# Retention and soft-MoE on one core: k by tokens made on the chip for ten steps, two weight pairs in ring tiles

## The chip, the cores and the metric

One NeuronCore of a Trainium2 chip runs the whole program. The metric is device time in microseconds (us), shorter is better. The engines are TensorE (PE, matmuls and transposes), VectorE (DVE), ScalarE (ACT), GpSimd (POOL) and SyncE (SP), which issues all DMAs here. Matmul results land in eight PSUM banks, everything else lives in SBUF.

## What is computed

```
# attention: q, k, v of 4 batches x 8 heads x 768 tokens x 64
state = gamma[h] * state + outer(k[t], v[t])      # per batch and head, 64 x 64
y[t]  = scale * q[t] @ state
x = y as (3072 tokens, 512)
# soft mixture of experts: 8 experts, 4 slots each
logits = x @ phi                                  # 3072 x 32
d = softmax over tokens;  slot_input = d.T @ x    # 32 x 512
h = relu(slot_input[e] @ w1[e]); slot_out[e] = h @ w2[e]    # 512 -> 1024 -> 512
c = softmax over slots;   out = c @ slot_out      # 3072 x 512
```

All data is fp32. The inputs are 25 MB of q, k, v (k twice: transposed and by tokens) and 33.6 MB of weights; the output is 6.3 MB.

## The kernel before, in words

The recurrence is done in chunks of 128 tokens. A step (NSTEP is 24) is one chunk of one batch with all 8 heads; step i belongs to batch i % 4. The main loop runs over P, 12 pairs of steps 2P and 2P+1. A group g is four steps, so two P.

**Inputs of a step.** load_in(i) (L169) takes one of six input tiles (NIN, 8 KB per partition) and loads four blocks of 512 columns: kT (k with head dimension on partitions), qT, v by tokens, and kn, k by tokens. The last four steps need no kn, as no state follows them; the first two load theirs late (L420). The scores are kT against qT, the state update is kn against v.

**Order on PE in one P** (P from 1 on). carry_mm (L215): the old states times q, from P = 2 on. attend_mm (L232): masked scores times v, into banks Y0 and Y1. state_mm (L259): kn times v into bank S, until P = 9. natural_mm (L276): eight transposes of the step outputs to token order, into A2 and A3. In even P turn_mm (L329), in odd P dispatch_u (L349, into A0) and logits_mm (L292, into sm). Then score_mm (L200) of the next two steps: 2P+2 into A0 and A1, 2P+3 into A2 and A3. P = 0 has its own order (L458 to L470): score_mm(2), attend, state_mm(0), score_mm(3), natural_mm(0) into A0 and A1. Before the loop stand score_mm(0), attend of step 0 and score_mm(1), with a few warm matmuls.

**Other engines.** VectorE masks the scores (L212), copies half of the step outputs (L257) and adds the state (L274); for P = 0 and 1, where the state begins, it copies it (L272). ScalarE copies the other half (L256), the transposed outputs (natural_copy, L288) and does the exponentials. GpSimd multiplies q (L191) and v (L195) by decay factors in place, as soon as a step's inputs are there.

**Order of the work.** manual_schedule (L93) keeps each engine's instructions in the order in which the program names them. A tile of a pool is given again once its last reader is done, and the instruction that writes it next waits for that. SP is one such ordered queue: a DMA that waits for its tile holds those behind it.

**Weights.** The list of weight tiles (L146) is 16 tiles of w1 and 16 of w2, 1 MB each, in the order of their use. PACE[P] of them are asked for at the head of each P, before that P's two inputs. The pool big holds 13; from P = 10 on weights go into input tiles that the last steps leave (weight_pool, L445), and after the loop into big again, each as a hidden-layer matmul frees it. The PACE of before asks for 19 tiles in the loop. The ring (NRING, nine tiles of 4 KB per partition) holds masked scores, step outputs and other short-lived data.

**After the loop.** hidden(g, k) (L558) does the first expert layer in eight pieces and frees two weight tiles with each; load_weights(2) stands behind each. Then the second layer (L654 to L663) in three blocks of output columns, and finish (L620), in which the 3072 x 512 output is made and stored by twelve DMAs of 512 KB (L646).

Of the kernel before, what the change touches and what calls it, by code (L numbers as in the profile page):

```python
# [43 lines left out]
NRING = 9  # L44
PACE = (1, 1, 1, 1, 1, 2, 1, 1, 2, 2, 2, 4)

# [34 lines left out]
def retention_soft_moe_kernel(  # L81
# [44 lines left out]
    cnat = small("cnat", [128, NSTEP, NSLOT])  # L126
    sst = [small(f"sst{b}", [128, NPAIR, D]) for b in range(B)]

# [21 lines left out]
    def load_weights(n):  # L150
        for _ in range(n):
            if not weights:
                return
            which, e, k = weights.pop(0)
            t = large(weight_pool[0])
            if which == "w1":
                nc.sync.dma_start(t, w1[e // 2, k])
                w1t[e, k], w1t[e + 1, k] = t[:, 0:FF], t[:, FF:2 * FF]
            else:
                nc.sync.dma_start(t, w2[w2n[0]])  # L160
                w2n[0] += 1
                w = BLOCKS[k][1]
                for j in range(256 // w):
                    w2t[e + j, k] = t[:, j * NFC * w:(j + 1) * NFC * w]

    st = {}
    pr = {}

    def load_in(i):  # L169
        t = large(inp)  # L170
        st[i] = dict(kT=t[:, 0:512].rearrange("p (g t) -> p g t", t=C),
                     qT=t[:, 512:1024].rearrange("p (g t) -> p g t", t=C),
                     v=t[:, 1024:1536].rearrange("p (h e) -> p h e", e=D),
                     kn=t[:, 1536:2048].rearrange("p (h d) -> p h d", d=D))
        if i < 2:
            if i == 0:
                nc.sync.dma_start(t[:, 0:1024], in_[i, :, 0:1024])
                nc.sync.dma_start(kt[:, 0:K_FIRST], consts[:, 0:K_FIRST])
                nc.sync.dma_start(t[:, 1024:1536], in_[i, :, 1024:1536])
            else:  # L180
                nc.sync.dma_start(t[:, 0:1536], in_[i, :, 0:1536])
            st[i]["late"] = (t[:, 1536:2048], in_[i, :, 1536:2048])
        elif i >= NSTEP - B:
            nc.sync.dma_start(t[:, 0:1536], in_[i, :, 0:1536])
        else:
            nc.sync.dma_start(t, in_[i])

    def decay_q(i):
# [79 lines left out]
    def state_add(P):  # L268
        for k in range(2):
            d = sst[(2 * P + k) % B]  # L270
            if P < B // 2:
                nc.vector.tensor_copy(d, pr[P]["S"][:, k])  # L272
            else:
# [123 lines left out]
    def split_c(q):  # L397
# [4 lines left out]
        nc.vector.tensor_tensor(c4r[:, :, :, 1, :], cq, c4s[q][:, :, :, 0, :], ALU.subtract)  # L402
        c4T[q] = slot()

# [14 lines left out]
    load_in(2)  # L419
    for i in range(2):  # L420
        nc.sync.dma_start(*st[i]["late"])
    load_in(3)
# [12 lines left out]
    score_mm(1)  # L435
    score_mask(1)
    for P in range(NPP):
        last = P == NPP - 1
# [19 lines left out]
        if P == 0:  # L458
# [7 lines left out]
            score_mask(3)  # L466
            natural_mm(0, names=("A0", "A1"))
            natural_copy(0)
            decay_table(qtab, K_QT)
            continue  # L470
        carry_mm(P)
        if last:
            dispatch_u(g - 1, ["A0"])
            logits_mm(g, (0, 1))
        attend_mm(P)
        if last:
            break
        attend_copy(P)
        if P < NPP - B // 2:
            state_mm(P)  # L480
            state_add(P)
        natural_mm(P)
        natural_copy(P)
# [236 lines left out]
```

## Time and profile before

| | us |
|---|---|
| median of 3 runs | 166.05 |
| all runs | 166.58, 166.05, 164.49 |
| the profiled execution | 164.77 |
| its span (first to last instruction) | 163.0 |
| PE busy | 146.4 (90%) |
| weight loads on PE (PEld) | 108.4 (67%) |
| DVE, ACT, POOL busy | 88.2, 39.1, 57.5 |
| DMA | 64.63 MB, mean 396 GB/s |

The span is what the rows of the profile divide; the profiled execution's own time is 1.77 us longer. Busy time of PE is that of modelled, pipelined instructions: the duration of one matmul overlaps the next, so the distance between starts is what a matmul costs in a row of them.

### The profile page before, as it was taken

What the parts mean: (1) busy time and instruction counts of PE and PEld (TensorE: products, weight loads), DVE (VectorE), ACT (ScalarE), POOL (GpSimd) and SP (SyncE); (2) the same over time, 40 slices, a digit from 0 to 9 for tenths busy, and PEclk for the clock granted to TensorE, in tenths of its full rate; (3) what the DMA queues carried; (4) which work ended last, traced back from release to release, by engine and by line L of the source; (5) the groups of instructions that cost most, each with busy time, mean ns of one, the idle gap of its engine ahead of it and who ended that gap; (6) DMA issues with size and microseconds to landing.
All of it is one profiled execution on the core that took longest, in us unless ns stands there. A gap on an engine that the chain in (4) does not pass through costs nothing.

```text
span 163.0 us, 5416 instructions
## 1 busy us (share of the span) xinstructions
PE 146.4 (90%) x2378; PEld 108.4 (67%) x2378; DVE 88.2 (54%) x198; ACT 39.1 (24%) x91; POOL 57.5 (35%) x62
## 2 busy tenths in 40 slices
PE   8976999999999899999999899999999999998400
PEld 2556989997999599869997787743244666565200
DVE  0437547574758675967576748677420305662500
ACT  3000222324332133122412332422114001432300
POOL 0231476858496666383885460000000000000000
PEclk9999999999999999999999999999999999999965
DMA  4899999999999999999999999998999999999993
GB/s 138 322 422 408 420 418 422 414 424 416 416 418 416 414 420 416 420 418 416 413 412 419 417 416 420 416 390 292 402 422 428 430 414 416 418 396 415 418 420 124
DMA packets 10679, 64.63 MB, mean 396 GB/s; under 512 B 1184, under 2 KB 1568, under 8 KB 4256
## 3 DMA queue, kind: packets, MB, share of 16 engines
q1 hardware_dynamic: 10656, 64.29, 96.5%
q8 instruction: 18, 0.29, 0.7%
q14 instruction: 5, 0.04, 0.1%
HBM read 58.00 MB, written 6.29 MB: 394 GB/s over the span
## 4 chain that ended last, share of the span: by engine, by line
PE 62%; DMA 22%; SPq 3%; DVE 2%; POOL 2%; issue 2%; ACT 1%; DVEq 0%; ACTq 0%; POOLq 0%
DMA b<-in_x_dram 16%; PE A L205 10%; PE Y L237 9%; PE A L660 7%; PE A L281 6%; DMA out_dram<-b 6%; PE Y L563 4%; PE Y L228 4%; PE S L265 4%; PE sm L298 3%; PE A L563 2%; PE S L563 2%; PE A L355 2%; PE A L410 2%; DVE r L212 2%
## 5 line engine op out<-in xcount | busy, mean ns | idle before, releaser
L212 DVE TENSOR_TENSOR r<-A,kt 128x512 f32<-128x512 f32 x48 | 30.0, 684 | 22.3 <-PE A L205 22.3
L191 POOL TENSOR_TENSOR b<-b,qtab 128x512 f32<-128x512 f32 x20 | 25.7, 1283 | 26.4 <-DMA b<-in_x_dram 19.5
L195 POOL TENSOR_TENSOR b<-b,kt 128x512 f32<-128x512 f32 x24 | 24.6, 1044 | 12.6 <-DMA b<-in_x_dram 12.6
L205 PE MATMUL A<-b 64*128 64x128 f32 x384 | 25.7, 282 | 3.6 <-DMA b<-in_x_dram 2.4
L205 PEld LDWEIGHTS A<-b 64*128 64x128 f32 x384 | 23.1, 191 | 6.8 <-issue 4.1
L237 PE MATMUL Y<-r,b 128*64 128x128 f32 x368 | 23.0, 276 | 0.0
L237 PEld LDWEIGHTS Y<-r,b 128*64 128x64 f32 x368 | 19.8, 137 | 2.5 <-issue 2.0
L288 ACT COPY r<-A 128x512 f32<-128x512 f32 x23 | 12.4, 589 | 29.3 <-PE A L281 29.3
L660 PE MATMUL A<-b,r 128*32 128x128 f32 (+1 forms) x384 | 16.3, 311 | 0.3 <-DMA b<-in_w_dram 0.3
L660 PEld LDWEIGHTS A<-b,r 128*32 128x32 f32 x384 | 10.7, 109 | 6.5 <-issue 2.9
L281 PE MATMUL A<-kt,r 128*128 128x128 f32 x96 | 13.3, 280 | 0.8 <-ACT r L256 0.8
L281 PEld LDWEIGHTS A<-kt,r 128*128 128x128 f32 x96 | 10.2, 140 | 2.2 <-ACT r L256 1.2
L265 PE MATMUL S<-b 128*64 128x64 f32 x320 | 11.0, 222 | 0.0
L265 PEld LDWEIGHTS S<-b 128*64 128x64 f32 x320 | 10.7, 138 | 0.0
L228 PE MATMUL Y<-b,sst 64*64 64x128 f32 x304 | 10.6, 276 | 0.0
L257 DVE COPY r<-Y 128x512 f32<-128x512 f32 x9 | 6.2, 690 | 5.9 <-PE Y L237 5.9
L228 PEld LDWEIGHTS Y<-b,sst 64*64 64x64 f32 x304 | 8.2, 132 | 1.2
L387 POOL TENSOR_TENSOR cnat<-cnat,cz 128x128 f32<-128x128 f32 x6 | 2.4, 401 | 17.2 <-DVE cz L386 10.4
L298 PEld LDWEIGHTS sm<-r,phis 128*32 128x32 f32 x192 | 6.2, 110 | 3.3 <-issue 3.3
L563 PE MATMUL Y<-b,siT 128*32 128x512 f32 x64 | 8.2, 597 | 0.0
L298 PE MATMUL sm<-r,phis 128*32 128x128 f32 x192 | 7.4, 273 | 0.0
L379 ACT ACTIVATE cnat<-cnat 128x128 f32<-128x128 f32 x6 | 1.9, 310 | 23.0 <-DVE cnat L378 23.0
(133 smaller groups left out, 158.4 us busy)
## 6 DMA issues: line engine op xcount, KB each, us to landing
b<-in_w_dram SPq DMA_DIRECT2D x32, 1024.0 KB, 16.9
b<-in_x_dram SPq DMA_DIRECT2D x18, 1024.0 KB, 13.6
out_dram<-b SPq DMA_DIRECT2D x12, 512.0 KB, 9.7
b<-in_x_dram SPq DMA_DIRECT2D x5, 768.0 KB, 13.8
b<-in_x_dram SPq DMA_DIRECT2D x3, 256.0 KB, 8.9
b<-in_x_dram SPq DMA_DIRECT2D x1, 512.0 KB, 4.3
kt<-in_consts_dram SPq DMA_DIRECT2D x1, 136.0 KB, 4.2
kt<-in_consts_dram SPq DMA_DIRECT2D x1, 116.0 KB, 6.7
```

The lines of the kernel that those rows point to most:

```text
L191: nc.gpsimd.tensor_tensor(q, q, qtab, ALU.mult)
L195: nc.gpsimd.tensor_tensor(v, v, vsc[:, i // B, :].unsqueeze(2).broadcast_to([128, H, D]), ALU.mult)
L205: nc.tensor.matmul(s["sc"][r][:, g, :], s["kT"][half(r), g, :], s["qT"][half(r), g, :], start=True, stop=True, skip_group_check=True)
L212: nc.vector.tensor_tensor(s["A"][:, r], s["sc"][r], mask.unsqueeze(1).broadcast_to([128, NPAIR, C]), ALU.mult)
L228: nc.tensor.matmul(p["y"][k][b][half(half_of(r, g)), gl, :], sst[(2 * P + k) % B][half(r), g, :], s["qT"][half(r), g, :], start=(gl == 0 a ...
L237: nc.tensor.matmul(pr[P]["y"][k][g // 2][half(half_of(r, g)), g % 2, :], s["v"][:, 2 * g + r, :], s["A"][:, r, g, :], start=(P < B // 2 an ...
L265: nc.tensor.matmul(S_[half(r), k, g, :], s["kn"][:, 2 * g + r, :], s["v"][:, 2 * g + r, :], start=True, stop=True, skip_group_check=True)
L281: nc.tensor.transpose(X[k][:, g * 128:(g + 1) * 128], pr[P]["yT"][:, k, g, :], ident)
L288: (nc.scalar.copy if engines[k] == "scalar" else nc.vector.tensor_copy)(xn, pr[P]["X"][k])
L298: nc.tensor.matmul(q["ltp"][32 * j:32 * j + 32, :], phis[:, p, :], st[GRP * g + j]["yT"][:, p, :], start=(p == 0), stop=(p == NPAIR - 1), ...
L563: nc.tensor.matmul(hp[g][hf][32 * j:32 * j + 32, :], siT[:, k, :], w1t[4 * g + j, k][:, hf * 512:(hf + 1) * 512], start=(k == 0), stop=(k ...
L660: nc.tensor.matmul(op[32 * j:32 * j + 32, :w], hT[fc // 4][:, fc % 4, 4 * g + j, :], t[:, fc * w:(fc + 1) * w], start=(g == 0 and fc == 0) ...
```

## The change

For the ten steps in TURNED, kn is no longer loaded; four PE transposes turn kT into a PSUM bank and one ScalarE copy writes kn (turn_k). Steps 0 and 1 are turned before the loop, 2 and 3 in P = 0 around natural_copy(0), and 4, 6, 8, 10, 12 and 14 in P = 1 to 6, between the state update and natural_mm. PACE is another sequence: 13 tiles until P = 8, none in P = 9, two each in P = 10 and 11. In P = 11 two more weight tiles are loaded as four halves into ring tiles (load_halves), and two into input tiles. The four states become slices of one tile, which c4T[0] takes over later. The first states (P = 0 and 1) are copied by ScalarE instead of VectorE.

```
--- before.py
+++ after.py
@@ -42,7 +42,8 @@
 NBIG = 13
 NIN = 6
 NRING = 9
-PACE = (1, 1, 1, 1, 1, 2, 1, 1, 2, 2, 2, 4)
+PACE = (1, 1, 2, 1, 2, 1, 2, 1, 2, 0, 2, 2)
+TURNED = (0, 1, 2, 3, 4, 6, 8, 10, 12, 14)
 
 K_MASK, K_VSC, K_YT, K_FIRST = 0, 128, 176, 272
 K_ID, K_QT, K_GC, K_J, K_ALL = 272, 400, 496, 500, 504
@@ -124,7 +125,8 @@
     wsel = small("wsel", [128, NSLOT])
     siT = small("siT", [128, NK, NSLOT])
     cnat = small("cnat", [128, NSTEP, NSLOT])
-    sst = [small(f"sst{b}", [128, NPAIR, D]) for b in range(B)]
+    sall = small("sst", [128, B * NPAIR * D])
+    sst = [sall[:, b * NPAIR * D:(b + 1) * NPAIR * D].rearrange("p (g e) -> p g e", e=D) for b in range(B)]
 
     ident = kt[:, K_ID:K_ID + 128]
     mask = kt[:, K_MASK:K_MASK + C]
@@ -161,7 +163,19 @@
                 w2n[0] += 1
                 w = BLOCKS[k][1]
                 for j in range(256 // w):
-                    w2t[e + j, k] = t[:, j * NFC * w:(j + 1) * NFC * w]
+                    for fc in range(NFC):
+                        w2t[e + j, k, fc] = t[:, (j * NFC + fc) * w:(j * NFC + fc + 1) * w]
+
+    def load_halves(n):
+        for _ in range(n):
+            _, e, k = weights.pop(0)
+            assert k == 0
+            for h in range(2):
+                t = slot()
+                nc.sync.dma_start(t, w2[w2n[0], :, h * 1024:(h + 1) * 1024])
+                for fc in range(4):
+                    w2t[e, k, 4 * h + fc] = t[:, fc * 256:(fc + 1) * 256]
+            w2n[0] += 1
 
     st = {}
     pr = {}
@@ -172,18 +186,20 @@
                      qT=t[:, 512:1024].rearrange("p (g t) -> p g t", t=C),
                      v=t[:, 1024:1536].rearrange("p (h e) -> p h e", e=D),
                      kn=t[:, 1536:2048].rearrange("p (h d) -> p h d", d=D))
-        if i < 2:
-            if i == 0:
-                nc.sync.dma_start(t[:, 0:1024], in_[i, :, 0:1024])
-                nc.sync.dma_start(kt[:, 0:K_FIRST], consts[:, 0:K_FIRST])
-                nc.sync.dma_start(t[:, 1024:1536], in_[i, :, 1024:1536])
-            else:
-                nc.sync.dma_start(t[:, 0:1536], in_[i, :, 0:1536])
-            st[i]["late"] = (t[:, 1536:2048], in_[i, :, 1536:2048])
-        elif i >= NSTEP - B:
+        if i == 0:
+            nc.sync.dma_start(t[:, 0:1024], in_[i, :, 0:1024])
+            nc.sync.dma_start(kt[:, 0:K_FIRST], consts[:, 0:K_FIRST])
+            nc.sync.dma_start(t[:, 1024:1536], in_[i, :, 1024:1536])
+        elif i in TURNED or i >= NSTEP - B:
             nc.sync.dma_start(t[:, 0:1536], in_[i, :, 0:1536])
         else:
             nc.sync.dma_start(t, in_[i])
+
+    def turn_k(i, name):
+        kp = bank(name)
+        for g in range(NPAIR):
+            nc.tensor.transpose(kp[:, g * 128:(g + 1) * 128], st[i]["kT"][:, g, :], ident)
+        nc.scalar.copy(st[i]["kn"], kp.rearrange("p (h d) -> p h d", d=D))
 
     def decay_q(i):
         q = st[i]["qT"]
@@ -269,7 +285,7 @@
         for k in range(2):
             d = sst[(2 * P + k) % B]
             if P < B // 2:
-                nc.vector.tensor_copy(d, pr[P]["S"][:, k])
+                nc.scalar.copy(d, pr[P]["S"][:, k])
             else:
                 nc.vector.tensor_tensor(d, d, pr[P]["S"][:, k], ALU.add)
 
@@ -400,7 +416,7 @@
         cq = cnat[:, 8 * q:8 * q + 8].unsqueeze(2).broadcast_to([128, 8, 2, NSLOT])
         nc.vector.tensor_copy(c4r[:, :, :, 0, :], cq)
         nc.vector.tensor_tensor(c4r[:, :, :, 1, :], cq, c4s[q][:, :, :, 0, :], ALU.subtract)
-        c4T[q] = slot()
+        c4T[q] = small("sst", [128, B * NPAIR * D]) if q == 0 else slot()
 
     c4p = {}
 
@@ -417,8 +433,6 @@
     load_in(1)
     nc.sync.dma_start(kt[:, K_FIRST:], consts[:, K_FIRST:])
     load_in(2)
-    for i in range(2):
-        nc.sync.dma_start(*st[i]["late"])
     load_in(3)
     nc.sync.dma_start(phis, phi)
     for i in range(4, NIN):
@@ -434,6 +448,8 @@
     attend_mm(0, [0])
     score_mm(1)
     score_mask(1)
+    turn_k(0, "S")
+    turn_k(1, "sm")
     for P in range(NPP):
         last = P == NPP - 1
         g = P // 2
@@ -465,13 +481,17 @@
             score_mm(3)
             score_mask(3)
             natural_mm(0, names=("A0", "A1"))
+            turn_k(2, "sm")
             natural_copy(0)
+            turn_k(3, "A0")
             decay_table(qtab, K_QT)
             continue
         carry_mm(P)
         if last:
             dispatch_u(g - 1, ["A0"])
             logits_mm(g, (0, 1))
+            load_halves(2)
+            load_weights(2)
         attend_mm(P)
         if last:
             break
@@ -479,6 +499,8 @@
         if P < NPP - B // 2:
             state_mm(P)
             state_add(P)
+        if 2 * P + 2 in TURNED:
+            turn_k(2 * P + 2, "A0")
         natural_mm(P)
         natural_copy(P)
         if P % 2 == 0 and P > 0:
@@ -656,9 +678,8 @@
         for g in range(2):
             for fc in range(NFC):
                 for j in range(4):
-                    t = w2t[4 * g + j, cb]
                     nc.tensor.matmul(op[32 * j:32 * j + 32, :w], hT[fc // 4][:, fc % 4, 4 * g + j, :],
-                                     t[:, fc * w:(fc + 1) * w],
+                                     w2t[4 * g + j, cb, fc],
                                      start=(g == 0 and fc == 0), stop=(g == 1 and fc == NFC - 1),
                                      skip_group_check=True, tile_position=(0, 32 * j))
                 if cb == 0 and g == 0 and fc == 2:
```

## Rows read from the trace of the kernel before

**Rows 1.** The page: busy time of PE, and DMA in 40 equal slices.

```profile
PE 146.4 (90%) x2378; PEld 108.4 (67%) x2378; DVE 88.2 (54%) x198; ACT 39.1 (24%) x91; POOL 57.5 (35%) x62
...
DMA  4899999999999999999999999998999999999993
GB/s 138 322 422 408 420 418 422 414 424 416 416 418 416 414 420 416 420 418 416 413 412 419 417 416 420 416 390 292 402 422 428 430 414 416 418 396 415 418 420 124
```

**Rows 2.** Windows: start:end, length, busy PE, PEld, DVE, ACT, POOL, PEclk, DMA share, GB/s.

```profile
108.00:114.00 6.00, 6.00 (x51) 1.89 (x53) 4.08 (x10) 0.90 (x2) 0.01 (x1) 1.00 0.83 314
110.00:111.00 1.00, 1.00 (x13) 0.42 (x13) 0.45 (x2) 0.00 (x0) 0.00 (x0) 1.00 0.45 188
153.00:156.00 3.00, 0.08 (x1) 0.00 (x0) 0.72 (x2) 0.71 (x2) 0.00 (x0) 1.00 1.03 421
156.00:157.00 1.00, 0.00 (x0) 0.00 (x0) 0.00 (x0) 0.00 (x0) 0.00 (x0) 0.67 1.02 418
157.00:158.00 1.00, 0.00 (x0) 0.00 (x0) 0.00 (x0) 0.00 (x0) 0.00 (x0) 0.50 1.02 418
```

**Rows 3.** The chain that ended last: start us, us, what.

```profile
104.16 0.44 PE A L410 x4
...
118.21 0.59 PE A L410 x4
...
142.91 9.50 DMA out_dram<-b
```

**Rows 4.** PE in order of time, start: start us, us, engine, line, operation [idle before].

```profile
9.55 1.16 PE L205 MATMUL A<-b 64*128 64x128 f32 x16
11.91 1.16 PE L205 MATMUL A<-b 64*128 64x128 f32 x16 [1.20 <-DMA b<-in_x_dram]
...
13.93 1.10 PE L265 MATMUL S<-b 128*64 128x64 f32 x32
16.27 1.16 PE L205 MATMUL A<-b 64*128 64x128 f32 x16 [1.24 <-DMA b<-in_x_dram]
17.36 1.09 PE L281 MATMUL A<-kt,r 128*128 128x128 f32 x8
18.38 1.97 PE L237 MATMUL Y<-r,b 128*64 128x128 f32 x32
```

**Rows 5.** GpSimd and ScalarE in order of time, the start.

```profile
11.84 1.04 POOL L195 TENSOR_TENSOR b<-b,kt 128x512 f32<-128x512 f32 x1 [1.75 <-DMA b<-in_x_dram]
...
16.20 1.04 POOL L195 TENSOR_TENSOR b<-b,kt 128x512 f32<-128x512 f32 x1 [3.31 <-DMA b<-in_x_dram]
...
18.05 1.07 ACT L288 COPY r<-A 128x512 f32<-128x512 f32 x2 [16.04 <-PE A L281]
```

**Rows 6.** ScalarE and PE in order of time, later P and the second layer.

```profile
45.61 1.07 ACT L288 COPY r<-A 128x512 f32<-128x512 f32 x2 [1.01 <-PE A L281]
...
46.16 2.06 PE L205 MATMUL A<-b 64*128 64x128 f32 x32
...
55.78 2.06 PE L205 MATMUL A<-b 64*128 64x128 f32 x32 [0.81 <-POOL cnat L387]
...
69.03 1.09 PE L281 MATMUL A<-kt,r 128*128 128x128 f32 x8 [0.24 <-ACT r L256]
...
72.25 2.06 PE L205 MATMUL A<-b 64*128 64x128 f32 x32 [0.26 <-issue]
...
146.66 0.63 PE L660 MATMUL A<-b,r 128*32 128x128 f32 x12 [0.26 <-DMA b<-in_w_dram]
```

**Rows 7.** SP in order of time: issues merged over the waits between them.

```profile
84.86 7.88 SPq L157 DMA_DIRECT2D b<-in_w_dram  x3
...
152.72 2.59 SPq L646 DMA_DIRECT2D out_dram<-b  x3
```

**Rows 8.** Groups of instructions: count, busy us, mean ns of one, idle before.

```profile
L288 ACT COPY r<-A 128x512 f32<-128x512 f32 x23 | 12.4, 589 | 29.3 <-PE A L281 29.3
...
L281 PE MATMUL A<-kt,r 128*128 128x128 f32 x96 | 13.3, 280 | 0.8 <-ACT r L256 0.8
```

More of the change, by code (lines that the diff above doesn't have):

```diff
@@ L126, in retention_soft_moe_kernel @@
     cnat = small("cnat", [128, NSTEP, NSLOT])
-    sst = [small(f"sst{b}", [128, NPAIR, D]) for b in range(B)]
+    sall = small("sst", [128, B * NPAIR * D])
+    sst = [sall[:, b * NPAIR * D:(b + 1) * NPAIR * D].rearrange("p (g e) -> p g e", e=D) for b in range(B)]
     ident = kt[:, K_ID:K_ID + 128]
@@ L163, in load_weights, with load_halves @@
                 for j in range(256 // w):
-                    w2t[e + j, k] = t[:, j * NFC * w:(j + 1) * NFC * w]
+                    for fc in range(NFC):
+                        w2t[e + j, k, fc] = t[:, (j * NFC + fc) * w:(j * NFC + fc + 1) * w]
+    def load_halves(n):
+        for _ in range(n):
+            _, e, k = weights.pop(0)
+            assert k == 0
+            for h in range(2):
+                t = slot()
+                nc.sync.dma_start(t, w2[w2n[0], :, h * 1024:(h + 1) * 1024])
+                for fc in range(4):
+                    w2t[e, k, 4 * h + fc] = t[:, fc * 256:(fc + 1) * 256]
+            w2n[0] += 1
     st = {}
@@ L174, in load_in @@
                      kn=t[:, 1536:2048].rearrange("p (h d) -> p h d", d=D))
[L175 to L183, printed above, removed]
+        if i == 0:
+            nc.sync.dma_start(t[:, 0:1024], in_[i, :, 0:1024])
+            nc.sync.dma_start(kt[:, 0:K_FIRST], consts[:, 0:K_FIRST])
+            nc.sync.dma_start(t[:, 1024:1536], in_[i, :, 1024:1536])
+        elif i in TURNED or i >= NSTEP - B:
             nc.sync.dma_start(t[:, 0:1536], in_[i, :, 0:1536])
@@ L186, in load_in, with turn_k @@
             nc.sync.dma_start(t, in_[i])
+    def turn_k(i, name):
+        kp = bank(name)
+        for g in range(NPAIR):
+            nc.tensor.transpose(kp[:, g * 128:(g + 1) * 128], st[i]["kT"][:, g, :], ident)
+        nc.scalar.copy(st[i]["kn"], kp.rearrange("p (h d) -> p h d", d=D))
     def decay_q(i):
@@ L271, in state_add @@
             if P < B // 2:
-                nc.vector.tensor_copy(d, pr[P]["S"][:, k])
+                nc.scalar.copy(d, pr[P]["S"][:, k])
             else:
@@ L419, in retention_soft_moe_kernel @@
     load_in(2)
-    for i in range(2):
-        nc.sync.dma_start(*st[i]["late"])
     load_in(3)
@@ L436, in retention_soft_moe_kernel @@
     score_mask(1)
+    turn_k(0, "S")
+    turn_k(1, "sm")
     for P in range(NPP):
@@ L467, in retention_soft_moe_kernel @@
             natural_mm(0, names=("A0", "A1"))
+            turn_k(2, "sm")
             natural_copy(0)
+            turn_k(3, "A0")
             decay_table(qtab, K_QT)
@@ L481, in retention_soft_moe_kernel @@
             state_add(P)
+        if 2 * P + 2 in TURNED:
+            turn_k(2 * P + 2, "A0")
         natural_mm(P)
```

10 lines of the change are left out of this document (6 added, 4 removed).

## The prediction

> **What bounds the kernel now.** I read the engine shares and slices first [rows 1], then the windows by stage and at the end [rows 2], the chain of waits [rows 3], and the instructions in order of time at the places that the change touches [rows 4 to 7]. There are two candidates. The DMA engines move 408 to 424 GB/s in nearly every slice from the third to the last but one, except for a dip around 106 to 114 us [rows 1]; in 108 to 114 us they carry 314 GB/s instead of about 418, which is 6 x 104 = 0.62 MB not moved, or 1.5 us [rows 2]. TensorE (PE) is busy 90% of the span [rows 1], and from 16.27 us to its last matmul at 153.1 us it hardly ever waits: the waits that I find in the stages that matter are 0.81, 0.24, 0.26 and 0.26 us [rows 6]. After the last matmul the DMAs need another 7 us for output that piled up behind the weights: they still run at 418 GB/s in 157 to 158 us, and the chain ends in a stretch "DMA out" of 9.50 us [rows 2, 3]. So PE paces the recurrence and the two expert layers, and a backlog of some microseconds on the DMA queue stands behind it. Bytes taken away shorten the backlog; columns put on PE move everything behind them. The change does both.
>
> **Bytes removed.** Ten steps lose the 128 x 512 block of k by tokens, 256 KB each: 2.62 MB, at 418 GB/s 6.3 us of DMA. The halves and the new pacing move no bytes in sum: 21 weight tiles instead of 19 are asked for before the first hidden layer, 11 instead of 13 after it.
>
> **Transposes added.** 40 transposes in ten groups of four. Eight take 1.02 us from start to the next instruction on PE (17.36 to 18.38, [rows 4]), so a group is 0.51 us; groups of four stand at 0.44 and 0.59 us in the chain [rows 3]. Ten groups: 5.1 us, bounds 4.4 and 5.9. Their own mean duration is 280 ns [rows 8], but they overlap in the pipe; 40 x 0.28 = 11.2 us would be the far end, and the row that shows eight back to back decides against it.
>
> **The start, groups 1 to 4.** PE now leaves score_mm(1) at about 10.6 us (9.55 plus 1.0) and waits until 11.91 for step 2 [rows 4]; GpSimd's v multiply of step 2 starts at 11.84, of step 3 at 16.20, when they land [rows 5]. Step 2 becomes 0.26 MB shorter: it lands 0.6 us earlier, at 11.2. Before step 3 four blocks go (the two late ones, step 2's and its own): 1.05 MB, 2.5 us, so 13.7. With turn_k(0) and (1), score_mm(2) starts at 10.6 + 1.02 = 11.6 instead of 11.91. score_mm(2), attend and state_mm keep their lengths, and score_mm(3) follows at 14.55 without the wait that now ends at 16.27. The eight transposes of natural_mm(0) run 15.6 to 16.65 (they run 17.36 to 18.38), and turn_k(2) to 17.15. Now a new wait: turn_k(3) writes bank A0, which natural_mm(0) has just filled, and ScalarE copies in program order: first kn of step 2, then A0. ScalarE starts its copy 0.18 us after the fourth transpose and takes 0.54 us per copy in a pair (18.05, two in 1.07, [rows 5]): kn 17.33 to 17.87, A0 to 18.41, so PE stands still from 17.15 to about 18.5, 1.35 us. turn_k(3) ends at 19.0, and the attend of P = 1 starts there instead of at 18.38: 0.62 us late. The bounds of this wait are 0 (nothing forces it on a chip if the copies came in the other order) and 2 us (if the copy of kn waits for a third copy of 0.59, [rows 8]); the code's order says 1.35. Behind turn_k(3) the whole of PE is queued.
>
> **P = 1 to 6, groups 5 to 10.** Each puts 0.51 us between state_mm and natural_mm, where PE has no slack: 3.06 us. On ScalarE each adds a copy of 0.59 us [rows 8], ten in all, ahead of natural_copy; ScalarE is busy 24% [rows 1]. The limit is score_mm(2P+3), which needs the banks of natural_copy: natural copies run 45.61 to 46.68, and its second half starts about 47.15, one microsecond after 46.16 [rows 6]. With the extra copy started 0.5 us sooner than the natural ones could have been, they end at the same distance from natural_mm, so about 0.5 us stays. I take nothing, with 0.3 us per group (the overrun if ScalarE comes one copy late, less part of that slack) as the upper bound, 1.8 us. The copies of the first states leave VectorE for ScalarE, four in all, beside state_mm and logits: nothing, bounds plus or minus 0.4 us.
>
> **Waits that go.** In P = 5 PE waits 0.81 us before score_mm [rows 6], behind VectorE's accumulate and GpSimd, which had itself waited for the inputs of a late DMA. Steps 12 and 13, which it uses, have nine shortened loads in or before them (9 x 0.63 = 5.6 us) and one weight tile more (2.5 us): they land 3.1 us sooner, and PE asks for them later. For the steps 14 to 19 the same count gives 1.3 to 3.8 us sooner. The group of P = 5 fills 0.51 us of this wait anyway: minus 0.81. The waits of 0.24 and 0.26 us in P = 7 have VectorE and ScalarE in them; I take half, minus 0.28 (bounds 0 and 0.5). The wait of 0.26 us at 146.66 for the last weights goes [rows 6].
>
> **Sum on PE.** 0.62 + 3.06 - 0.81 - 0.28 - 0.26 = 2.3 us: the last matmul at 155.4 instead of 153.1. Bounds: with groups of 0.44 (0.7 less), a new wait of 0.8 (0.55 less) and the waits of P = 7 all gone, 0.8; with groups of 0.59 (0.8 more), the 1.8 us for ScalarE and none of the wait of P = 5 recovered but what the group fills (0.3 more), about 5.2.
>
> **The DMA side.** The backlog runs out sooner. All inputs, the constants and the first 13 weight tiles are 38.1 MB now, at 418 GB/s and with the 3.7 us that the first slices lose [rows 1] through at about 95 us; with 35.5 MB it is 89. The next two tiles wait for input buffers freed at state_mm(9), whose loads now go out at 84.86, and the two after them for attend_mm(10) (the three issues of 84.86 to 92.74, [rows 7]), both 2.3 to 2.9 us later. So a gap of 2 to 3 us opens near 95 us, another of 2 to 3 us before the first hidden layer frees a tile, against the one gap of 1.5 now. The halves come too late for the first and share the second: two ring slots are free at once, two only after dispatch_u(4). DMA alone would end 6.3 - 3.1 = 3.2 us earlier (a net 3.1 us of new gaps), but it cannot store what PE has not made. The last three outputs are 1.57 MB, 3.8 us. Their issues lie between 152.72 and 155.31 now, the later ones held up by the queue [rows 7]; shifted by 2.3 the first goes at 155.0, and with 1.0 us from issue to bytes (an estimate: the window 110 to 111, in which the first issue after the dip falls, carries 188 GB/s [rows 2]; bounds 0.5 and 2) the last bytes move at 155.0 + 1.0 + 3.8 = 159.8. In the kernel before they end at about 160.1, counted at full rate. So 0.3 us is gained: span 162.7 against 163.0.
>
> The profiled execution took 164.77 us for its span of 163.0, 1.28 below the median of 166.05. On its scale the forecast is 164.4; a median of runs may lie anywhere from there to 1.3 above, and I take the middle: **165.1 us**. Any PE delay moves this one to one, so by the bounds 0.8 and 5.2 it lies between 163.6 and 168.0. About 2% is what a measurement of this kernel can tell from no change.
>
> **A rule weighed.** Eight transposes in a row take 1.02 us among other matmuls [rows 4]; PE's granted clock was 1.00 in 153 to 156 us and 0.50 after 157, PE having finished at 153.1 [rows 2]. The Trainium skill, "TensorE: Matmul & The Clock Gate", Part 4, says that transposes don't count as PE work for the clock, and gives about 275 ns for one in a kernel. By its price the groups would cost an estimated 11 us instead of 5.1. The row of eight disagrees with that price as a rate; a stretch of transposes alone no run here shows. What such a clock would do here is the third rival below.
>
> **Rivals.** (1) DMA bounds the kernel after all: for it speak its share near 1.0 throughout and the 7 us of backlog [rows 1, 2]. Then PE's delay hides and only the gaps count: 163.0 - 3.2 = 159.8, so 161.6 on the profiled scale and about 162.2 as a median, 2.3% faster. Against it: PE has no idle time to hide 40 transposes in. "Perfetto Trace Analysis" of the Trainium skill, Identifying the Most-Contended Engine, would have PE judged by weight loads, 67% of the span here, which speaks for this rival; the chain says otherwise [rows 3].
> (2) Slower by ScalarE: the copy of kn holds bank A0 or delays natural_copy in each P from 1 to 6, and PE waits at score_mm. The point is the 0.5 us of slack above; if the wait is 0.6 to 0.9 us (one copy and a bit), six times, 3.6 to 5.4 us: 168.7 to 170.5, slower by 1.6 to 2.7%.
> (3) Slower by the clock: PE does only transposes and a wait from 15.6 to 19.0 us. The only fall in the trace comes after PE has stopped [rows 2], which speaks against it; no stretch of this kind is there to speak for it. At 1.2 GHz the work that follows takes twice as long. Two P take 72.25 - 55.78 = 16.5 us [rows 6], so if the low clock lasts through the work of one P it costs 8 us, and through the half of one 4. I price it at 4: 169.1.
> (4) The change doesn't do what it says: the gap is not filled because SP is in order. That is already in the forecast, since DMA has 3 us to spare at the end.
>
> **Chances.** Forecast 0.66, rival 1 0.16 (half of it beyond 2%), rival 2 0.12, rival 3 0.06. The range reaches from rival 1 to the lower end of rivals 2 and 3: 162.0 to 168.7. Faster by over 2% 0.10, within 2% 0.75, slower by over 2% 0.15 (most of rivals 2 and 3, and mishaps of the forecast that reach 169.4).
>
> **What would show it.** Right: PE idle before the transposes on A0 of step 3 at about 17 us, 1.2 to 1.5 us; no DMA wait at score_mm(2) and (3); 0.5 us more in each P from 1 to 6, save P = 5; last matmul near 155.4; DMA gaps near 95 and 113 us; and output that follows the last matmul within 5 us instead of 7. Wrong: a last matmul at or before 153.5, a wait at score_mm in P = 1 to 6, a clock below 1.00 near 20 us, or an unbroken DMA stream to the end.

## The result, and the profile after

The changed kernel takes 163.55 us (median of 11 runs, 162.69 to 164.04); the kernel before, in the same comparison, 166.05 us (11 runs, 164.49 to 167.08). The ratio is 0.987 with the interval [0.9835, 0.9905]: 1.3% faster, within the 2% band. The forecast was 165.1 us, range 162.0 to 168.7, "within 2%" the likeliest. The profiled executions are nearer to each other than the medians: 163.85 us with a span of 162.0, against 164.77 and 163.0. Where the text subtracts times of rows, it goes by these. Ratios leave out the few runs that were slow in either kernel; the medians given are of all runs.

The page of the changed kernel: busy time, the DMA slices and the chain by engine.

```profile
PE 150.6 (93%) x2418; PEld 112.5 (69%) x2418; DVE 81.7 (50%) x194; ACT 45.6 (28%) x105; POOL 57.2 (35%) x62
...
PEclk9999999999999999999999999999999999999995
DMA  5899999999999999999999978999799999999976
GB/s 139 330 401 428 415 427 415 417 415 421 421 417 416 419 415 419 415 413 417 414 417 374 333 253 340 337 391 427 247 421 427 429 415 421 417 386 408 359 291 253
...
q8 instruction: 19, 0.31, 0.8%
...
PE 86%; DMA 3%; DVE 3%; issue 2%; ACT 1%; POOL 1%; SPq 0%; DVEq 0%; ACTq 0%; POOLq 0%
```

Beside [rows 1]: PE is busy 4.2 us more (40 matmuls more), the queue moves 2.6 MB less and has lost its evenness in two places, in slices 22 to 26 and in slice 29, and the last three slices no longer run full. The chain is now PE for 86%; before, it ended in a DMA stretch [rows 3].

PE in order of time at the start (start us, us, engine, line, operation, idle before), which answers to [rows 4].

```profile
9.19 1.16 PE L221 MATMUL A<-b 64*128 64x128 f32 x16
...
11.33 1.16 PE L221 MATMUL A<-b 64*128 64x128 f32 x16
...
14.38 1.16 PE L221 MATMUL A<-b 64*128 64x128 f32 x16
...
16.40 0.60 PE L201 MATMUL sm<-kt,b 128*128 128x128 f32 x4
18.16 0.65 PE L201 MATMUL A<-kt,b 128*128 128x128 f32 x4 [1.17 <-ACT r L304]
```

And ScalarE in the same stretch, which answers to [rows 5].

```profile
17.04 0.58 ACT L202 COPY b<-sm 128x512 f32<-128x512 f32 x1 [1.90 <-PE sm L201]
17.52 1.08 ACT L304 COPY r<-A 128x512 f32<-128x512 f32 x2
```

score_mm(2) and (3) (L221 at 11.33 and 14.38) follow without a wait; the 1.20 and 1.24 us for inputs are gone. In their place PE stands 1.17 us before the transposes of step 3: ScalarE copies kn first (17.04), the natural banks second (17.52), and bank A0 is free only then.

PE in order of time later on: P = 1, P = 4 and 5, the first hidden-layer matmul, the last matmul.

```profile
20.55 1.10 PE L281 MATMUL S<-b 128*64 128x64 f32 x32
21.58 0.66 PE L201 MATMUL A<-kt,b 128*128 128x128 f32 x4
...
27.07 1.97 PE L253 MATMUL Y<-r,b 128*64 128x128 f32 x32
...
45.57 1.09 PE L281 MATMUL S<-b 128*64 128x64 f32 x30
47.04 0.33 PE L281 MATMUL S<-b 128*64 128x64 f32 x2 [0.38 <-issue]
47.30 0.66 PE L201 MATMUL A<-kt,b 128*128 128x128 f32 x4
47.79 1.04 PE L297 MATMUL A<-kt,r 128*128 128x128 f32 x8
...
53.79 0.57 PE L281 MATMUL S<-b 128*64 128x64 f32 x13
55.26 0.80 PE L281 MATMUL S<-b 128*64 128x64 f32 x19 [0.90 <-issue]
55.99 0.66 PE L201 MATMUL A<-kt,b 128*128 128x128 f32 x4
...
111.97 1.06 PE L585 MATMUL A<-b,siT 128*32 128x512 f32 x8
...
155.62 0.50 PE L664 MATMUL A<-r 128*128 128x512 f32 x1
```

In the kernel before, the attend of P = 2, which ends P = 1, starts here:

```profile
26.26 1.97 PE L237 MATMUL Y<-r,b 128*64 128x128 f32 x32
```

From the start of a group of transposes to the next instruction it is 0.49 us (47.30 to 47.79). What a group adds to its P is a little less: from attend to attend, P = 1 takes 8.32 us (18.75 to 27.07) against 7.88 before (18.38 to 26.26), so 0.44. The waits of [rows 6] at score_mm in P = 5 and 7, at natural_mm in P = 7 and for the last weights are gone. Two stops stand there instead that name no engine ("issue"), 0.38 and 0.90 us, in the middle of state_mm. By the distance between starts they cost more: a state_mm without a stop takes 1.03 us to the next instruction (20.55 to 21.58), these two 1.73 (45.57 to 47.30) and 2.20 (53.79 to 55.99), so 0.70 and 1.17, together 1.87 us.

DMA windows (start:end, length, busy time of five engines, clock, DMA share, GB/s): the two holes, and the end.

```profile
96.00:98.00 2.00, 1.44 (x23) 1.16 (x20) 0.86 (x3) 1.26 (x5) 0.00 (x0) 1.00 0.38 66
...
115.00:116.00 1.00, 1.00 (x13) 0.16 (x6) 0.88 (x1) 0.15 (x1) 0.00 (x0) 1.00 0.20 66
...
159.00:160.00 1.00, 0.00 (x0) 0.00 (x0) 0.00 (x0) 0.00 (x0) 0.00 (x0) 0.50 1.05 426
160.00:161.00 1.00, 0.00 (x0) 0.00 (x0) 0.00 (x0) 0.00 (x0) 0.00 (x0) 0.50 0.45 172
161.00:162.00 1.00, 0.00 (x0) 0.00 (x0) 0.00 (x0) 0.00 (x0) 0.00 (x0) 0.50 0.00 0
```

The same view of the end of the kernel before, further on than [rows 2] show it.

```profile
159.00:160.00 1.00, 0.00 (x0) 0.00 (x0) 0.00 (x0) 0.00 (x0) 0.00 (x0) 0.50 0.75 307
160.00:161.00 1.00, 0.00 (x0) 0.00 (x0) 0.00 (x0) 0.00 (x0) 0.00 (x0) 0.50 0.36 147
161.00:162.00 1.00, 0.00 (x0) 0.00 (x0) 0.00 (x0) 0.00 (x0) 0.00 (x0) 0.50 0.05 20
```

**The time in two pieces.** Let H be the start of the first hidden-layer matmul. Before, H stands at 108.30, and the span ends 54.7 us later. After, H stands at 111.97 (3.67 us late), and the span ends 50.0 us later (4.7 us less). The gain of 1.0 us in the profile is the difference of two moves of four or five microseconds. The table has both pieces for all kernels; "4, first" means that natural_copy(0) also stands ahead of turn_k(2). The rate is the DMA's in the window 85 to 120 us, in which 35 us at 418 GB/s would be a full queue. H and what is counted from it come from one profiled execution of each kernel; the spans of a kernel's timed runs lie 0.8 to 2.3 us apart, so differences of less than a microsecond between two rows are weak. The profiled execution of e10 is one of its longest: span 164.0, where the median of its twelve is 162.75.

| run | steps turned | pacing | halves | MB | GB/s 85:120 | H | H to last matmul | H to end | ratio to before |
|---|---|---|---|---|---|---|---|---|---|
| before | 0 | old | no | 64.63 | 398 | 108.30 | 44.28 | 54.7 | 1 |
| after | 10 | new | yes | 62.02 | 344 | 111.97 | 43.65 | 50.0 | 0.987 |
| e1 | 0 | new | yes | 64.64 | 404 | 113.16 | 43.66 | 50.1 | 0.997 |
| e2 | 10 | old | no | 62.02 | 325 | 113.44 | 44.55 | 54.4 | 1.021 |
| e3 | 10, first | new | yes | 62.02 | 362 | 110.65 | 43.65 | 50.1 | 0.983 |
| e4 | 10, twice each | new | yes | 62.02 | 330 | 115.53 | 43.65 | 50.1 | 1.013 |
| e5 | 4, first | new | yes | 63.60 | 408 | 109.89 | 43.64 | 50.3 | 0.984 |
| e6 | 7, first | new | yes | 62.81 | 383 | 109.95 | 43.65 | 50.5 | 0.981 |
| e7 | 10, kn loaded too | new | yes | 64.12 | 392 | 112.62 | 43.65 | 50.0 | 0.992 |
| e8 | 10 | new | no | 62.02 | 283 | 112.37 | 44.73 | 54.5 | 1.020 |
| e9 | 10 | old | yes | 62.02 | 368 | 112.82 | 43.66 | 50.6 | 1.000 |
| e10 | 0 | old | yes | 64.63 | 413 | 109.90 | 43.65 | 54.1 | 0.999 |
| e11 | 4, first | old | yes | 63.60 | 413 | 107.27 | 43.66 | 52.4 | 0.980 |
| e12 | 4, first | old | no | 63.60 | 391 | 106.73 | 44.30 | 54.1 | 0.987 |

### The profile page after: what moved, and what is told of

Read it like the earlier page. It is cut to its first block, busy times and chain, and to the rows that moved or that the text cites. A ratio compares the mean times of both kernels' runs of the same rounds, so it can differ in the third digit from the quotient of the medians.

```text
span 162.0 us, 5531 instructions
## 1 busy us (share of the span) xinstructions
PE 150.6 (93%) x2418; PEld 112.5 (69%) x2418; DVE 81.7 (50%) x194; ACT 45.6 (28%) x105; POOL 57.2 (35%) x62
## 2 busy tenths in 40 slices
DMA packets 10680, 62.02 MB, mean 383 GB/s; under 512 B 1184, under 2 KB 1568, under 8 KB 5536
## 4 chain that ended last, share of the span: by engine, by line
PE 86%; DMA 3%; DVE 3%; issue 2%; ACT 1%; POOL 1%; SPq 0%; DVEq 0%; ACTq 0%; POOLq 0%
PE A L221 14%; PE Y L253 12%; PE A L681 9%; PE A L297 7%; PE S L281 6%; PE Y L244 5%; PE Y L585 4%; PE sm L314 4%; PE A L371 3%; DMA b<-in_x_dram 3%; PE A L201 3%; PE A L585 2%; PE S L585 2%; PE A L664 2%; PE A L426 2%
## 5 line engine op out<-in xcount | busy, mean ns | idle before, releaser
L221 PE MATMUL A<-b 64*128 64x128 f32 x384 | 25.2, 279 | 0.3
L221 PEld LDWEIGHTS A<-b 64*128 64x128 f32 x384 | 22.6, 187 | 3.2 <-issue 1.6
L281 PE MATMUL S<-b 128*64 128x64 f32 x320 | 11.6, 222 | 1.3 <-issue 1.3
L338 ACT COPY lts<-sm 128x128 f32<-128x128 f32 x5 | 1.3, 266 | 23.9 <-DVE mg L335 19.7
L290 DVE TENSOR_TENSOR sst<-sst,S 128x256 f32<-128x256 f32 x16 | 6.0, 418 | 3.8 <-PE S L281 3.8
```

The lines of the kernel that those rows point to most:

```text
L221: nc.tensor.matmul(s["sc"][r][:, g, :], s["kT"][half(r), g, :], s["qT"][half(r), g, :], start=True, stop=True, skip_group_check=True)
L281: nc.tensor.matmul(S_[half(r), k, g, :], s["kn"][:, 2 * g + r, :], s["v"][:, 2 * g + r, :], start=True, stop=True, skip_group_check=True)
```

## The experiments

All are timed against the kernel before in five rounds, in four groups (e1 to e4, e5 to e7, e8 to e11, e12; the median of the kernel before was 165.1 to 165.4 in each); diffs are against the changed kernel. The changed kernel itself was timed in another group, where the kernel before took 166.05. All runs keep the copies of the first states on ScalarE, so what that part of the change does by itself is not shown.

**e1: no transposes.**

```
-TURNED = (0, 1, 2, 3, 4, 6, 8, 10, 12, 14)
+TURNED = ()
...
-    turn_k(0, "S")
-    turn_k(1, "sm")
```

(with the late loads of the first two steps, as before, and without turn_k(2) and (3))

> All of k by tokens is loaded as before, and PE gets no transposes; the pacing, the halves and the ScalarE copies of the first states stay. Theory A (PE paces up to the last matmul, and the DMA backlog behind it only fills what PE leaves): PE's last matmul stays at about 153 us, the gap of 1.5 us before the first hidden layer closes because two more weight tiles are queued, bytes in sum are unchanged, so 1 to 1.5 us faster than the kernel before (ratio 0.991 to 0.994). Rival B (bytes alone set the time): no change, 1.00. Rival C (each weight tile asked for early is worth its 2.5 us): 5 us faster, 0.97.

Measured: 164.99 us, ratio 0.9967 [0.9934, 1.0]. PE's waits by what ended them (us in total, times, longest):

```profile
PE A L221 <- POOL b L207: 2.8, 4, 1.3
PE A L221 <- DMA b<-in_x_dram: 2.6, 2, 1.5
PE A L221 <- POOL b L211: 1.1, 1, 1.1
PE A L221 <- POOL cnat L403: 0.9, 1, 0.9
```

All four are score_mm waiting for inputs, directly or by way of GpSimd, 7.4 us in all; the 2.6 us behind the DMA itself are at the start, where the kernel before has 2.4. PE does 40 transposes less and still reaches H 1.2 us later than in the changed kernel: with the new pacing weight tiles stand ahead of inputs. e10 below, the same kernel with the old pacing, reaches H 3.3 us earlier than e1. The expected gain of 0.6 to 0.9% was not there, since that price was left out of it; nor did a tile that comes early gain 2.5 us (rival C).

**e2: transposes without halves and pacing.**

```
-PACE = (1, 1, 2, 1, 2, 1, 2, 1, 2, 0, 2, 2)
+PACE = (1, 1, 1, 1, 1, 2, 1, 1, 2, 2, 2, 4)
...
-            load_halves(2)
-            load_weights(2)
```

> Ten steps are turned as in the change, but the pacing is that of before (19 tiles) and no halves are loaded. Theory A: PE reaches the first hidden layer 2.5 to 3.7 us later than before, and from there 13 tiles and the output, 19.9 MB or 47.8 us of DMA, remain as before; 2 to 3.5 us slower than the kernel before (ratio 1.012 to 1.02). Rival B: 6.3 us of bytes are gone, 3 to 6 us faster (0.965 to 0.98).

Measured: 168.85 us, ratio 1.0208 [1.0164, 1.0253]. Against the kernel before, H is 5.1 us later, and H to end stays at that of the kernel before, 54.4. The 2.6 MB that are not loaded buy nothing: the queue idles for them (385 GB/s from 20 to 85 us, where the kernel before has 418, and 325 from 85 to 120). By themselves the ten groups make the kernel 2% slower, near the upper end of what theory A expected; rival B, by which the bytes alone set the time, falls. H is later than theory A's 2.5 to 3.7 us. Three stops without an engine are in it, at 47.14, 55.63 and 82.64 us; by the starts of the P in which they stand they cost 0.7, 1.4 and 1.0 us.

**e3: the order of two copies.**

```
-            turn_k(2, "sm")
             natural_copy(0)
+            turn_k(2, "sm")
             turn_k(3, "A0")
```

> The changed kernel with natural_copy(0) ahead of turn_k(2) in the program, so that ScalarE empties bank A0 first. Theory A: the wait of 1.17 us before turn_k(3) is gone and every later PE instruction moves by it; 1.0 to 1.2 us faster than the changed kernel (ratio to before about 0.980). Rival B: the wait is covered by the DMA queue, no change against the changed kernel (0.987).

Measured: 162.57 us, ratio 0.9833 [0.9791, 0.9875]. PE in order of time:

```profile
16.28 0.60 PE L201 MATMUL sm<-kt,b 128*128 128x128 f32 x4
16.71 0.62 PE L201 MATMUL A<-kt,b 128*128 128x128 f32 x4
17.27 1.97 PE L253 MATMUL Y<-r,b 128*64 128x128 f32 x32
```

The wait is gone, attend of P = 1 starts 1.48 us earlier than in the changed kernel and H 1.3; H to end is the same 50.1. So in these two executions the wait of 1.2 us shows in full. The medians are 1.0 us apart, the ratios by 0.004, with intervals that overlap; the profile tells the two kernels apart, the timed runs barely.

**e4: each transpose twice.**

```
-        for g in range(NPAIR):
+        for g in 2 * list(range(NPAIR)):
```

> The changed kernel with each group of four transposes done twice into the same bank: 40 more transposes, no more bytes and copies. Theory A: 40 x 0.125 = 5 us more on PE, one to one in the time: 4 to 5 us slower than the changed kernel (about 168 us, ratio to before 1.01 to 1.018). Rival B: at most 1.5 us slower, as DMA hides the rest. If the granted clock depends on transposes, it falls below 1.00 in the stretch from 15 to 20 us and the loss is larger.

Measured: 167.35 us, ratio 1.0129 [1.009, 1.0168]. PE in order of time, a doubled group with its wait and what follows it, and then the window of 15 to 20 us (columns as above):

```profile
19.63 1.09 PE L201 MATMUL A<-kt,b 128*128 128x128 f32 x8 [1.16 <-ACT r L304]
20.65 0.55 PE L253 MATMUL Y<-r,b 128*64 128x128 f32 x6
```

```profile
15.00:20.00 5.00, 3.84 (x53) 3.41 (x48) 2.92 (x5) 2.15 (x5) 1.44 (x2) 1.00 1.00 415
```

Eight transposes take 1.02 us here. H moves by 3.56 us and the span by 3.6, a little under the 4 to 5 expected. Attend of P = 1 starts 1.90 us later, and doubling adds 0.43 to 0.44 us to each of P = 1 to 3 (0.93 instead of 0.49 for a group); with the same in P = 4 to 6 that is 4.5 us. The two stops of the changed kernel in P = 4 and 5, 1.87 us, are not there; in their place are one in P = 7 and a wait of 0.31 us for GpSimd in P = 6. So the columns on PE show in full, and the difference is the stops. Rival B falls, and the granted clock stays 1.00.

**e7: the bytes back, nothing added on PE.**

```
-        elif i in TURNED or i >= NSTEP - B:
+        elif i == 1 or i >= NSTEP - B:
```

> The changed kernel, but the eight steps 2, 3, 4, 6, 8, 10, 12 and 14 load their block of k by tokens as well as making it by transposes (which write over it): 2.1 MB of useless bytes, 5.0 us at about 417 GB/s, with no instruction added to TensorE. Theory A: TensorE starts P = 1 as late as the DMA waits at score_mm(2) and (3) make it (they return, about 1 us each, and take the place of the wait for ScalarE), inputs come late by up to 3 us around P = 3 to 5, and the tail gets the rest: last matmul 157 to 159, 165.5 to 167.5, ratio 1.00 to 1.015. Rival B: all 5 us show: 168.5, ratio 1.018. If the bytes are worth nothing because TensorE alone sets the time: 163.6, ratio 0.99.

Measured: 164.03 us, ratio 0.992 [0.9888, 0.9951]. 2.1 MB, 5.0 us of DMA, cost 0.6 us of span (162.6 against 162.0), and 0.5 of it is the start, where attend of P = 1 begins at 19.25 instead of 18.75. The window 85 to 120 us says where they went:

```profile
85.00:120.00 35.00, 33.86 (x504) 23.56 (x504) 25.73 (x62) 9.19 (x25) 11.07 (x12) 1.00 0.98 392
```

At 392 GB/s instead of 344 it carries 35 x 48 = 1.7 MB more: the bytes fill the hole that their removal had opened. Rival B falls again, and so does theory A's number: PE waits for inputs for 0.35 us at the start and, by way of GpSimd, for 0.58 us in P = 9, not for 3. That PE, with its transposes, asked for them later than in e1 is the likely reason; no run tests it by itself. The third case, in which bytes are worth nothing, is the nearest.

**e5 and e6: fewer transposed steps.**

```
-TURNED = (0, 1, 2, 3, 4, 6, 8, 10, 12, 14)
+TURNED = (0, 1, 2, 3)
```

(e6 has (0, 1, 2, 3, 4, 6, 8); both have the order of e3)

> Steps 4, 6, 8, 10, 12 and 14 load k by tokens again; only steps 0 to 3 make it by transposes, with the copy of A0 ahead of that of step 2 as in the run that put natural_copy first. Six groups of 0.49 us leave TensorE, 2.9 us, and 6 x 0.26 = 1.57 MB come back, 3.8 us at about 417 GB/s. Beside that run (ratio 0.983): theory A (TensorE paces up to its last matmul, and inputs come late only if the queue ahead of them grows by more than its slack) says that score_mm waits for late inputs return in P = 3 to 5 as in the run without any transposes, and take back 1.5 to 3 us of the 2.9: ratio 0.972 to 0.985, last matmul 151.5 to 153.5. Rival B (bytes set the time): 3.8 us slower than that run, ratio 1.00 to 1.01. Point between them: 0.99.

> Steps 10, 12 and 14 load k by tokens again; steps 0 to 4, 6 and 8 make it by transposes, with the copy of A0 ahead of that of step 2. Three groups leave TensorE (1.5 us), 0.79 MB come back (1.9 us of DMA). Theory A: the bytes come back behind the inputs that were late in the run without transposes, so TensorE keeps its 1.5 us or loses up to half of it to waits: ratio 0.973 to 0.980, last matmul 152.8 to 153.6. Rival B: 1.9 us slower than the run with ten groups in this copy order, ratio 0.990 to 0.997. Point between them: 0.985.

Measured: e5 162.93 us, 0.9843 [0.9796, 0.9889]; e6 162.25 us, 0.9808 [0.9768, 0.9848]. Neither is told apart from e3 (0.9833), and rival B's 1.00 and 0.99 did not come. From the attend of P = 1 to H it is 93.4 us in e3, 91.9 in e5 and 93.1 in e6. e5 keeps 1.5 of the 2.9 us taken from PE: score_mm waits for inputs again, by way of GpSimd, 1.0, 0.9 and 0.5 us, as theory A expected. e6 keeps 0.3 of 1.5, which theory A did not expect: it is 2.0 us ahead of e3 up to the attend of P = 7 and loses this again in P = 7, 8 and 9. The rows name one wait in each, 0.23 us behind ScalarE and two stops without an engine, 0.27 and 0.61 us; from attend to attend these P are 0.38, 0.44 and 0.87 us longer than in e3, which is the whole loss of 1.7.

**e8 and e9: without the halves; with the old pacing.** e8 drops the line load_halves(2); e9 takes the pacing of e2 and drops load_weights(2) alone.

> The changed kernel without the two pairs of halves (its pacing and its transposes stay, 19 weight tiles instead of 21 before the first hidden layer). Theory A2, from the runs so far: the span is the later of two ends, TensorE's last matmul plus 6.4 us (so in the changed kernel and in all its variants so far with halves) and the DMA's end, which is the bytes at 418 GB/s plus the stretches that the queue stands empty. Without the halves 2.1 MB (5.0 us) are asked for later, so the gap before the hidden layer grows by 2 to 5 us and the DMA's end passes TensorE's: span 163.5 to 165.5, last matmul within 0.5 us of 155.6, tail 8 to 10 us, ratio 0.996 to 1.010. Rival D, the halves do nothing (they wait for their slots too long) and the pacing gave the short tail: ratio 0.985 to 0.990, tail 6.4.

> The changed kernel with the pacing of the kernel before, halves and transposes as changed. Theory A2: the early gaps of the run without halves and with the pacing of before (span 167.8; 5 us of empty queue between 20 and 85 us, 7 in 100 to 120) stay in part, the halves fill up to 5.0 us of the second: span 163 to 165, ratio 0.992 to 1.005. Rival D (halves do nothing): span 167.8, ratio 1.02. Rival E (only the halves matter, the pacing nothing): span 162.0, ratio 0.987.

Measured: e8 168.41 us, 1.02 [1.0165, 1.0234]; e9 165.58 us, 1.0003 [0.997, 1.0036]. The window of e8:

```profile
85.00:120.00 35.00, 34.40 (x512) 23.89 (x512) 24.17 (x62) 9.47 (x26) 6.80 (x9) 1.00 0.74 283
```

283 against 344 GB/s is 2.1 MB, the two pairs of halves, or 5.1 us, and H to end grows by 4.5. The loss was larger than I had put it (1.02 instead of at most 1.010), since none of the hole closed again. Rival D falls. e9 has the time expected: with the old pacing the halves still keep H to end at 50.6, and H is 0.85 us later than in the changed kernel. The span is 1.4 us longer, so rival E, by which the pacing does nothing beside the halves, falls too.

**e10 to e12: which parts are needed.** e10 is e1 with the old pacing, e11 is e5 with the old pacing, e12 is e11 without halves.

```
-TURNED = (0, 1, 2, 3, 4, 6, 8, 10, 12, 14)
+TURNED = (0, 1, 2, 3)
...
-PACE = (1, 1, 2, 1, 2, 1, 2, 1, 2, 0, 2, 2)
+PACE = (1, 1, 1, 1, 1, 2, 1, 1, 2, 2, 2, 4)
...
-            load_weights(2)
```

(e11, beside the order of e3)

> The kernel before with the halves alone (and the copies of the first states on ScalarE): its pacing, all k by tokens loaded, no transposes. Theory A2: no byte goes, but the halves fill the gap of about 1.5 us before the hidden layer; TensorE is not the later end here (152.6 + 6.4 = 159.0 against 163.0), so the gain shows whole: span 161.5, ratio 0.988 to 0.994, last matmul within 0.5 us of 152.6, tail 9 us. Rival D: ratio 1.00. Rival F, TensorE alone sets the time and its tail follows it: span 163.0, ratio 1.00.

> The best of the reasons put together: transposes for steps 0 to 3 alone (where TensorE waited for inputs), A0 copied ahead of the kn of step 2, halves, and the pacing of the kernel before, so that no weight tile stands ahead of an input earlier than it did. Theory A2: 1.05 MB less (2.5 us), 1.5 us of gap filled: DMA ends at 159.0 to 161; last matmul 151.5 to 152.5, so 158 to 159 by TensorE. Span 159 to 161, ratio 0.972 to 0.985. If the pacing of the changed kernel is needed for the tail, span 162 or more and ratio 0.99.

> The run with four transposed steps, halves and the pacing of the kernel before (ratio 0.980), without the halves: what do the four early turns give by themselves? Theory A2: they take 1.05 MB (2.5 us) from the queue and start TensorE about 1.5 us earlier, but nothing is there to ask for the bytes that fit before the hidden layer, so the gap between 100 and 120 us grows from nearly none to 3 to 4 us and the DMA's end comes back to 162.5 to 163.5: ratio 0.990 to 1.000. Rival G, the halves do nothing here (alone they gave 0.999): ratio 0.978 to 0.984, span 160. Point between them: 0.987.

Measured: e10 164.97 us, 0.9991 [0.9961, 1.0021]; e11 162.01 us, 0.9804 [0.9771, 0.9837]; e12 162.96 us, 0.9874 [0.9828, 0.992]. e11 has the lowest median of all, below both kernels of this case, with four groups of transposes instead of ten and the old pacing; e3, e5 and e6 are not told apart from it. Four early transposed steps with the order of e3 (e12) give as much as the whole change. e12 lies between the ranges of theory A2 and rival G; beside it the halves of e11 are worth 1.1 us of span, not 4.9. The window 85 to 120 us of e10, and its end:

```profile
85.00:120.00 35.00, 33.51 (x458) 21.56 (x455) 23.03 (x56) 8.74 (x24) 9.21 (x11) 1.00 1.01 413
```

```profile
158.00:159.00 1.00, 0.00 (x0) 0.00 (x0) 0.00 (x0) 0.00 (x0) 0.00 (x0) 0.50 0.73 295
159.00:160.00 1.00, 0.00 (x0) 0.00 (x0) 0.00 (x0) 0.00 (x0) 0.00 (x0) 0.50 0.34 139
160.00:161.00 1.00, 0.00 (x0) 0.00 (x0) 0.00 (x0) 0.00 (x0) 0.00 (x0) 0.50 0.13 53
161.00:162.00 1.00, 0.00 (x0) 0.00 (x0) 0.00 (x0) 0.00 (x0) 0.00 (x0) 0.50 0.06 25
```

The hole is filled (413 GB/s), and full rate ends a microsecond earlier than in the kernel before, at about 158 us. But the last bytes then trickle out over more than four, the span of this execution is 164.0, and the expected 1% did not come. H is also 1.6 us later than in the kernel before, where theory A2 had the last matmul within 0.5 us: PE starts P = 1 0.4 us later, and a wait of 0.93 us behind GpSimd in P = 9 is the longest after that. As this execution is 1.25 us longer than the median of its kernel's spans, its rows may show more than the usual run has. Why the end is so ragged there was not tried.

## Why the prediction held, point by point

**What holds the end.** The text said that PE paces the recurrence and the expert layers with a DMA backlog behind it. Right, and the table sharpens it. From H to the last matmul PE takes 43.65 us in every run with halves, whatever else differs, and 44.3 to 44.7 without. H to end is 50.0 to 50.6 with halves wherever the queue once more ran short of work in the 4 us behind H (66 GB/s at 115 to 116 us in the changed kernel; the shallowest dip is that of e5, 279 GB/s at 113 to 114), and 54.1 to 54.7 without halves, whatever the bytes saved earlier. Without them 13 weight tiles and 12 outputs are left from there, 13.6 + 6.3 = 19.9 MB or 47.7 us at 418 GB/s, to which come the wait for the first tile to be freed and the ragged end; with them it is 11 tiles, 42.7 us, and PE ends last. In e10 and e11 the queue does not run short there; they move 20.4 MB behind H, the changed kernel 18.7, and lie at 54.1 and 52.4. They carry a backlog into this stretch.

**Transposes.** Ten groups were put at 0.51 us. The rows give 0.49 to the next instruction, but what a group adds to its P is 0.43 to 0.44 (P = 1 to 3), in e4 once more: the lower bound of 0.44 was the price. The six groups of the later P cost 2.6 us, not 3.06.

**The start.** A wait before turn_k(3) of 1.35 us was reckoned from the code's order: 1.17. P = 1 late by 0.62: by 0.37 (18.75 against 18.38). e3 shows that this wait, unlike the bytes, was worth its full size in the profiles.

**ScalarE.** Taken at nothing, and nothing it was: no score_mm waits for natural_copy. Rival 2 did not come.

**Waits that go.** The 0.81 in P = 5 and the 0.26 for the last weights went as said; of P = 7 both went (0.50, I had taken 0.28). The last matmul moved by 3.04 us (152.58 to 155.62), the forecast was 2.3. By distances between starts, up to H: start 0.37, six groups 2.64, two stops 1.87, less 0.88 in P = 5 and 0.52 in P = 7, and about 0.2 spread over other P, is 3.67, what H moved. Behind H PE takes 0.63 us less (44.28 against 43.65), 0.26 of it the wait for the last weights. The stops stood nowhere in my sum. It was near by luck: other terms had been set too high, and the stretch behind H gave back more than I had taken.

**The DMA side.** Two holes near 95 and 113 us were forecast; they stand at 96 to 98 and near 115. Mis-sized: 3.1 us of new gap. From 398 to 344 GB/s over 35 us it is 54 x 35 / 418 = 4.5 us, so of 6.3 us of bytes 1.8 are left, not 3.2. That changed nothing in the time, as e7 shows: DMA was no longer the later end. Rival 1 (162.2) falls: PE's delay did not hide. It had the sign right, for another reason, the shorter piece behind H. Rival 4 falls in e8: the halves do fill their place in time, and are worth 4.9 us of span there. I had said that the halves and the pacing move no bytes in sum and had left it at that; that they move them across H is the half of the change that pays. It pays where the queue would stand empty: with no transposes and the old pacing (e10) it pays nothing that these runs can tell.

**The end.** Last bytes at 159.8 and a span of 162.7 were forecast: they run to about 160.4, and the span is 162.0. From the end of the last matmul to the end of the span I had put 7.3 us (9.9 before): it is 5.9. So PE came 0.7 us later than forecast and the piece behind it was 1.4 us shorter. The step that failed is that I carried the distance from full rate's end to the end of the span (160.1 to 163.0) over from the kernel before. There it holds three us of falling rate, 307, 147, 20 GB/s; here the rate falls within one.

**From span to median.** I put the median 0.7 us above the profiled scale, as runs of the kernel before lie up to 1.3 above it. The median came 0.3 below its profiled execution: 1.0 of the 1.55 us by which 165.1 is too high, the rest being the span. The runs of the kernel before spread over 2.6 us, those after over 1.35, and a profiled execution near the low edge of one was compared with one near the high edge of the other. Why they spread differently stays open; it is not the tail on DMA alone, as e8 and e12 end on DMA as well and spread over 0.95 us.

**The clock.** The granted clock is 1.00, the higher of its two levels (2.4 GHz), in the stretch of transposes, even doubled (e4), so rival 3 did not come. The Trainium skill, "TensorE: Matmul & The Clock Gate", Part 4, says that transposes do not count as PE work for the clock, and gives about 275 ns for one. The 275 ns agree with the mean duration of one here, 280 ns [rows 8], but are not its price in a row, where eight take 1.02 us. Of the clock these runs show no loss; a longer stretch of transposes alone was not tried.

## What to carry to other kernels

Cut the span where the queue runs empty, and count on each side what is left: bytes saved before the last hole only widen it (2.1 MB were worth 0.6 us here), while bytes moved from behind it to ahead of it count in full as long as the hole takes them (2.1 MB were worth 4.9 us in e8, 1.1 in e11 beside e12, and nothing to be seen in e10, where the hole was small). Put replacement work on the pacing engine only where that engine stands still: the four groups at the start, where PE waited 2.4 us for inputs, did as much as ten, as far as these runs tell. And when a PSUM bank is used again, look at the order of the copies on the engine that empties it: two lines exchanged were worth 1.3 us of span in the profiles and 1.0 in the medians.

## What was unexpected of the hardware

PE stopped twice in the middle of state_mm without a semaphore, 0.38 and 0.90 us by the rows, 1.87 by starts. Between the two, 125 matmuls and as many weight loads ran, 250 instructions. In the trace's records a packet of the instruction queue (19 of 16 KB, the q8 row above) ends about 1.4 us before PE goes on in both cases.

The other kernels show the same. In the ten runs with transposed steps (the changed kernel, e2 to e9 and e11; e12 has none) there are 19 such stops inside state_mm or natural_mm. Each ends 1.3 to 1.5 us behind the end of such a packet. Counted in PE matmuls from the start of the trace, they stand at 726 to 727, 851 to 853, 1231, 1356 to 1358 and 1485, so about 126 or a multiple of 126 apart, whatever the pacing and the bytes. In e4, with more PE instructions ahead, the one stop that is left stands in another P (76.33 us), but on this count (1231). So the number of instructions ahead seems to place a stop, not the work around it. This looks like instructions coming late beside a full data queue (417 GB/s between the two stops).

The Trainium skill, "Runtime: NRT & Kernel Launch", Instruction fetch mechanics, has instructions come in blocks of 256 and the crossing mostly hidden; the spacing agrees, the hiding does not in these places. No run was made to settle the cause. Why some crossings stop PE and others do not stays open, and so does why the kernel before has but one stop, of 0.26 us ([rows 6], 72.25): it too stands 1.4 us behind a packet, but at 1201 matmuls.

The other surprise is the ragged end: in the kernel before and in e10, which reach their last microseconds with a backlog, the rate falls over three and five us; in the changed kernel, where the queue waits for PE's last output, it falls within one.
